# Two blocks' down projections joined into two levels of seven products, in a fused attention and SwiGLU kernel

## The chip, the cores and the metric

The kernel runs on one core of a Trainium2 chip. The metric is the device time of one execution in microseconds (us); a lower time is better. A profile shows one execution, and its span is the time from the first to the last instruction that the profiler saw.

## The reference

Attention without a softmax, normed by rows, feeds a SwiGLU feed-forward block. All is float32.

```python
kv = np.einsum('bhsd,bhse->bhde', k, v)          # 8 batches, 8 heads, 576 positions, 64 wide
out = np.einsum('bhsd,bhde->bhse', q, kv)
rms = np.sqrt(np.mean(out * out, axis=-1, keepdims=True) + 1e-06)
attn_out = out / rms * g_norm
x = attn_out.transpose(0, 2, 1, 3).reshape(4608, 512)
g = x @ w_gate                                   # 512 -> 1536
silu = g * (1.0 / (1.0 + np.exp(-g)))
result = (silu * (x @ w_val)) @ w_out            # 1536 -> 512
```

## The kernel before

The 4608 tokens are cut into nine blocks of 512. For each block, the attention makes x (transposed, features on the partitions), the *up phase* makes h = silu(x w_gate) * (x w_val), and the *down phase* makes h w_out. Matrix products are made by Strassen's scheme in Winograd's form: a product of 2 x 2 blocks takes seven block products, numbered 1 to 7, instead of eight, and sums and differences of blocks before and after. The names follow: `XO`, `XI`, `CHAIN` map a product's number to its operand and to its PSUM bank.

Blocks 0 to 2 go alone. Blocks 3 and 4, 5 and 6, 7 and 8 go in pairs (`Pair`). A pair's up phase (`Pair.up`, `Inner`) has two levels of seven products for both blocks at once. It runs in six steps j, one for each 256 columns of the gate and value weights (2 x 128 each). A step has the seven outer products in four groups: (1, 5), (6, 2), (7), (4, 3), called g0 to g3. Each group has seven inner products, and one of them is one matmul of 128x128 by 128x256 for each outer product in the group. A step has thus 49 matmuls. The 49 weights come from a DRAM tensor, `w`, through nine buffers `t` (`Stream.pump`), sent on SP's queue.

The inner products of a group share PSUM banks: 1, 6, 7 and 4 add up in a bank "b" (three buffers), 5 and 3 in a bank "c" (two), and 2 has a bank "a" (one). After each of them VectorE or ScalarE reads the bank, adds what is to be added, and writes a tile `r` in SBUF (L820 to L832); only then may the next product of the same bank begin. ScalarE does this for products 1, 5, 6 and 4 of g0, VectorE for all others. TensorE's order interleaves two groups: 1, 5, the last group's 3, 6, the last group's 4, 2, 7 (`Inner.sequence`, L798). GpSimd makes the outer sums (`made1` and `made2`: four sums of 128x256 and one of 128x1024 each step), and after g3's last product (`made3`, L852) two multiplies of 128x1024 that make h, and a sum and a difference of 128x256 for the first block of the pair (`h_sums`). In the sixth step VectorE makes the multiplies and these sums.

A block's down phase (`Ffn.down`, `Down`) has one level of seven products. Each has six steps of contraction and two row tiles: 12 matmuls of 128x128 by 128x256, h being the stationary operand, so that the output has tokens on the partitions and is stored in rows. The pair's two blocks go down one after the other, 14 products in all. The weights are quadrants of `wo` in SBUF and three differences, that GpSimd makes into `t` buffers (`turn_t`, L997). In the last two blocks (`lone`) product 3 comes ahead of 4 and has a bank "m"; in the last block (`final`) its halves are apart, one ahead of product 4 and one behind it, and each half is summed and stored by itself. The second block's sums of h are made by GpSimd during the first one's down phase (`second_sums`, L1252).

The order of the work is that of the program, which a scheduler lays out by priorities for each engine; `tc.issue_after(x)` puts what follows behind an instruction x in that order, and `in_order` (L135) fixes the program's order for the engines named. Each engine takes its own queue strictly in turn.

Of the kernel before, what the change touches and what calls it, by code (L numbers as in the profile page):

```python
# [14 lines left out]
P = 128  # L15
# [3 lines left out]
def kernel(  # L19
# [114 lines left out]
    @contextmanager  # L134
    def in_order(*engines):  # L135

        traced = nc.cur_bb.bb.instructions
        last = traced[-1]
        yield
        start = next(k for k in reversed(range(len(traced))) if traced[k] is last) + 1  # L140
        before = {}
        for i in traced[start:]:
            if engines and i.engine not in engines:
                continue
            if i.engine in before:
                tc.add_manual_dep(
                    i, before[i.engine].name,
                    mybir.DependencyInfo(mybir.DependencyClass.NoSync, mybir.DependencyReason.DATA), reason="order",
                )
            before[i.engine] = i  # L150

# [488 lines left out]
    class Quad:  # L640


        def __init__(self, steps):
            self.steps = steps
            self.ps, self.room = {}, None

            self.apart = {}

# [3 lines left out]
        def multiply(self, p):  # L652
            name, first = CHAIN[p]
            if first:
                tiles = [PSUMS[name].tile([P, 2, HB], F32, name=name) for _ in range(1 + (name in self.apart))]
                self.ps[name], self.apart[name] = tiles[0], tiles[-1]
            banks = self.ps[name], self.apart[name]
            for e, i in self.order(p):
                lhsT, rhs = self.operands(p, e, i)

                self.ffn.multiplied = nc.tensor.matmul(  # L661
                    banks[e][:, e], lhsT=lhsT, rhs=rhs, start=first and i == 0 and (e == 0 or banks[0] is not banks[1]),
                    stop=i == self.steps - 1, skip_group_check=True,
                )
            getattr(self, f"after{p}", lambda: None)()
# [91 lines left out]
    class Inner:  # L757
# [94 lines left out]
        def made3(self, p, e, q):  # L852
            if p != 4:
                return
            h = h_both[:, :, 2 * self.j : 2 * self.j + 2]
            halves = lambda t: t.rearrange("p (b e) t -> p b e t", b=2)
            c11, c12, c21, c22 = (self.whole(*i) for i in ((1, 1), (3, 1), (3, 0), (1, 0)))

            engine = nc.gpsimd if self.j + 1 < NP else nc.vector
            mul(engine, h[:, :, :, 0:HB], halves(c11), halves(c12))  # L860
            with tc.issue_after(self.ffn.fifth.ins):
                nc.scalar.activation(out=c21, in_=c21, func=ACT.Silu)
            mul(engine, h[:, :, :, HB:BLK], halves(c21), halves(c22))
            self.ffn.ended = self.ffn.a.h_sums(self.j, 1, engine)

# [13 lines left out]
    class Stream:  # L879
# [15 lines left out]
        def pump(self):  # L895

            while self.next and not self.held[-9]:
                n, j, c = key = self.next.pop(0)
                tile_ = t_tile(key)
                os, ps = JOINT[c]  # L900
                count = len(os) * len(ps)
                self.tiles[key] = tile_.rearrange("p a (b c) -> p (a b) c", c=P)
                self.uses[key] = count
                to = self.tiles[key][:, 0:count].rearrange("p (o i) c -> p o (i c)", o=len(os))
                src = self.dram[:, j, steps_of(OUTERS, os), steps_of(INNERS, ps)].rearrange("p o i c -> p o (i c)")
                nc.sync.dma_start(out=to, in_=src)

        def use(self, n, j, o, p):
            c, i = self.joint[o, p]
            key = n, j, c  # L910
            self.uses[key] -= 1
            if not self.uses[key]:
                self.free(key)
            return self.tiles[key][:, i]
# [4 lines left out]
    stream = Stream()  # L919
# [65 lines left out]
    class Down(Quad):  # L985
        def __init__(self, ffn):
            super().__init__(NP)
            self.ffn = ffn
            self.t = {}
            self.final = ffn.n == NB - 1  # L990
            self.lone = False
            self.opens = None
            self.keeps = False
            if self.final:
                self.apart["c"] = None
# [16 lines left out]
        def multiply(self, p, es=(0, 1)):  # L1012
            if p == 3 and self.lone:
                self.third(es)
                return
# [7 lines left out]
        def third(self, es):  # L1023


            if es[0] == 0:
                tiles = [m_psum.tile([P, 2, HB], F32, name="m") for _ in range(1 + self.final)]
                self.thirds = tiles[0], tiles[-1]
            for e in es:
                for i in range(self.steps):  # L1030
                    lhsT, rhs = self.operands(3, e, i)
                    self.ffn.multiplied = nc.tensor.matmul(  # L1032
                        self.thirds[e][:, e], lhsT=lhsT, rhs=rhs, start=i == 0 and (e == 0 or self.final),
                        stop=i == self.steps - 1, skip_group_check=True,
                    )
            if not self.final:
                add(nc.vector, self.o1[:, :, HD:DM], self.thirds[0], self.u2)
                self.ffn.store(self.o1, 0)
                return
            for e in es:  # L1040
                add(nc.vector, self.o1[:, e, HD:DM], self.thirds[e][:, e], self.u2[:, e])
                self.ffn.store(self.o1[:, e : e + 1, HD:DM], e, slice(HD, DM))

        def after6(self):
            super().after6()
            if self.lone:
                self.add_c(self.u2, self.u2)

        def order(self, p):
            order = [(e, i) for e in range(2) for i in range(self.steps)]  # L1050
            return order if p == 3 and self.final else sorted(order, key=lambda ei: ei[1])
# [17 lines left out]
        def rows(self):  # L1069
            o = ring()  # L1070
            self.o1, self.o2 = o[:, 0:2], o[:, 2:4]

        def after2(self):
            if self.lone:
                self.rows()
            add(nc.vector, self.o1[:, :, 0:HD], self.ps["a"], self.s)
            if self.final:
                self.ffn.store(self.o1[:, :, 0:HD], 0, slice(0, HD))
# [4 lines left out]
        def after7(self):  # L1083
            if not self.lone:
                self.rows()
            u3 = self.piece(2)
            nc.scalar.copy(out=u3, in_=self.ps["b"])
            self.add_c(self.o2[:, :, HD:DM], u3)
# [5 lines left out]
        def after3(self):  # L1094
            self.add_c(self.o1[:, :, HD:DM], self.u2)
            if not self.final:
                self.ffn.store(self.o1, 0)
                return
            for e in range(2):
                self.ffn.store(self.o1[:, e : e + 1, HD:DM], e, slice(HD, DM))  # L1100

        def add_c(self, o, u):

            if not self.final:
                add(nc.vector, o, self.ps["c"], u)
                return
            for e, c in enumerate((self.ps["c"], self.apart["c"])):
                add(nc.vector, o[:, e], c[:, e], u[:, e])

    class Ffn:  # L1110
# [9 lines left out]
        def store(self, o, t, columns=slice(None)):  # L1120
            rows = out[BLK * self.n : BLK * (self.n + 1), columns].rearrange("(t p) d -> p t d", t=T)
# [40 lines left out]
        def down(self, nxt, then={}):  # L1162
# [3 lines left out]
            down.lone = nxt is None  # L1166
            order = (1, 6, 5, 7, 2, 4, 3) if 5 in fill else (1, 5, 6, 7, 2, 4, 3)
            if down.lone:
                order = (1, 5, 6, 2, 7, 3, 4)
            for p in order:  # L1170
# [5 lines left out]
                with tc.issue_after(nxt.multiplied.ins) if self.n == 0 and p in (5, 6) else ExitStack():  # L1176
                    down.multiply(p, *[(0,)] * (p == 3 and down.lone and down.final))
# [14 lines left out]
            if down.lone and down.final:  # L1192
                down.multiply(3, (1,))
# [25 lines left out]
    class Pair:  # L1219


        def __init__(self, n):
            self.n = n
            self.a, self.b = (Ffn(i, blocks[i]) for i in (n, n + 1))
            self.visited = None

        def up(self, fill):

            a = self.a
            a.s1 = s_pool.tile([P, NP, HB], F32, name="s1")  # L1230
# [5 lines left out]
            for i, this in enumerate(units):  # L1236
                for unit, p in this.sequence(last):
                    if unit:
                        visited, self.visited = self.visited, None
                        with tc.issue_after(visited.ins) if visited else ExitStack():  # L1240
                            unit.multiply(p)
                last = this
                fill.get(i + 1, lambda: None)()
            a.down_ = Down(a)
            a.down_.keeps = True
            a.down_.turn_t(5)
# [3 lines left out]
            a.ended = self.ended  # L1250
# [165 lines left out]
    for n in range(PAIRED, NB, 2):  # L1416
# [3 lines left out]
        if after:  # L1420
# [10 lines left out]
            for i in range(8):  # L1431
                fill[12 + i] = lambda i=i, after=after: after[i // 4].load_quarters(i % 4 // 2, (i % 2,))
        pair.up(fill)
        if after:
            after[0].turn()
        if len(after) > 2:
            after[2].load_kv(0)
        with in_order(nc.tensor.engine):
            pair.a.down(after[0] if after else None, {5: pair.second_sums})
            if after:  # L1440
                after[1].turn()
            if len(after) > 2:
                after[2].load_kv(1)
            pair.b.down(after[1] if after else None)
# [31 lines left out]
```

## Time and profile before

| | us |
|---|---|
| median of three runs | 1012.57 (1011.34 to 1013.79) |
| the profiled execution, its own time | 1012.7 |
| its span | 1010.9 |
| TensorE busy | 993.7 (98%) |
| VectorE busy | 673.7 (67%) |
| GpSimd busy | 369.6 (37%) |
| ScalarE busy | 232.2 (23%) |
| last up phase (blocks 7 and 8), from about 808 to | 934.85 |
| the two down phases behind it, to TensorE's last matmul | 1007.55 |

In the profile PE is TensorE, PEld its weight loads, DVE is VectorE, ACT is ScalarE, POOL is GpSimd and SP is the engine whose queue sends most of the DMAs. A row of a group of instructions gives the line of the code, the engine, the operation, the tile written and the tiles read, the shape and the count; most sums have the lines of three helpers, L130 (add), L131 (subtract) and L132 (multiply). A matmul of float32 shows as two records. A transfer's "us to landing" is the time from its issue to the arrival of its data.

### The profile page before, as it was taken

Reading aid. Unit: us, or ns where it says so; the run is one execution under the profiler, and the core shown is the slowest. Engines: PE = TensorE matmul, PEld = TensorE weight load, DVE = VectorE, ACT = ScalarE, POOL = GpSimd, SP = SyncE. Lnnn points to the kernel's source line nnn. Section 1 sums busy time; section 2 is a strip of 40 time slices with the busy share of each in tenths; the row PEclk is TensorE's granted clock in tenths of the full one; section 3 lists DMA queues with packets and bytes.
Section 4 is the critical chain, followed back from the end, with each engine's and each line's share of the span. In section 5 each row is a group of like instructions: output and inputs, shape, how many; then the busy total and the mean of one; then the engine's idle time right before and its main releaser. Section 6 shows DMA issues by size and latency. Waiting matters only on the chain.

```text
span 1010.9 us, 17078 instructions
## 1 busy us (share of the span) xinstructions
PE 993.7 (98%) x6506; PEld 831.6 (82%) x6506; DVE 673.7 (67%) x1121; ACT 232.2 (23%) x367; POOL 369.6 (37%) x290
## 2 busy tenths in 40 slices
PE   5999999999999999999999999999999999999998
PEld 4544688888888888888888888888888888888887
DVE  2999797589868477656676746666668566666311
ACT  2665111221122311212211121121112121121000
POOL 0000263255544240445456004455660026546600
PEclk9999999999999999999999999999999999999999
DMA  8688653483866855767742464667221654553011
GB/s 220 198 266 260 120 93 136 97 288 97 210 136 122 214 114 158 189 179 182 170 130 42 111 164 135 182 164 191 77 42 43 146 164 144 150 145 101 1 42 42
DMA packets 254290, 143.23 MB, mean 142 GB/s; under 512 B 149504, under 2 KB 236544, under 8 KB 254208
## 3 DMA queue, kind: packets, MB, share of 16 engines
q1 hardware_dynamic: 223488, 138.20, 50.8%
q10 hardware_dynamic: 30656, 3.94, 2.5%
q8 instruction: 52, 0.85, 0.4%
q14 instruction: 30, 0.25, 0.1%
q0 software_dynamic: 64, 0.00, 0.0%
HBM read 104.99 MB, written 28.70 MB: 132 GB/s over the span
## 4 chain that ended last, share of the span: by engine, by line
PE 75%; DMA 1%; POOL 0%; SPq 0%; issue 0%; DVE 0%; POOLq 0%
PE b L816 22%; PE b L661 20%; PE c L816 11%; PE c L661 9%; PE a L816 5%; PE a L661 5%; PE m L431 1%; PE m L1032 1%; PE m L370 1%; DMA ld<-in_v_dram 1%; POOL t L131 0%; SPq L312 0%; PE b L370 0%; PE b L431 0%; PE a L431 0%
## 5 line engine op out<-in xcount | busy, mean ns | idle before, releaser
L816 PE MATMUL b<-arena,t 128*128 128x256 f32 x1008 | 244.5, 381 | 0.0
L816 PEld LDWEIGHTS b<-arena,t 128*128 128x128 f32 x1008 | 190.1, 190 | 29.6 <-DVE r L130 2.4
L130 POOL TENSOR_TENSOR r<-r 128x256 f32<-128x256 f32 (+1 forms) x90 | 94.7, 1054 | 246.1 <-DVE r L130 154.9
L130 DVE TENSOR_TENSOR r<-b,r 128x512 f32<-128x512 f32 (+1 forms) x234 | 138.9, 606 | 60.1 <-PE b L816 54.8
L130 DVE TENSOR_TENSOR r<-c,r 128x512 f32<-128x512 f32 (+1 forms) x170 | 104.5, 623 | 81.9 <-PE c L816 40.1
L132 POOL TENSOR_TENSOR arena<-r 128x1024 f32<-128x1024 f32 (+1 forms) x54 | 102.1, 1904 | 112.3 <-DVE r L130 67.9
L131 POOL TENSOR_TENSOR t<-wo 128x512 f32<-128x512 f32 x54 | 76.9, 1445 | 167.8 <-DVE wo L130 105.9
L130 DVE TENSOR_TENSOR r<-a,r 128x512 f32<-128x512 f32 x93 | 59.2, 636 | 108.3 <-PE a L661 70.7
L816 PE MATMUL c<-arena,t 128*128 128x256 f32 x504 | 122.5, 379 | 0.0
L131 DVE TENSOR_TENSOR arena<-arena 128x512 f32<-128x512 f32 (+3 forms) x96 | 104.3, 1101 | 20.0 <-PE b L661 17.7
L816 PEld LDWEIGHTS c<-arena,t 128*128 128x128 f32 x504 | 95.6, 190 | 13.5 <-issue 0.3
L661 PE MATMUL b<-wo,arena 128*128 128x256 f32 x432 | 98.1, 382 | 0.2
L661 PE MATMUL b<-t,arena 128*128 128x256 f32 x432 | 96.2, 379 | 0.0
L661 PEld LDWEIGHTS b<-wo,arena 128*128 128x128 f32 x432 | 81.2, 190 | 12.5 <-DVE arena L132 0.9
L661 PEld LDWEIGHTS b<-t,arena 128*128 128x128 f32 x432 | 82.1, 190 | 11.2
L830 ACT COPY r<-b 128x512 f32<-128x512 f32 x54 | 31.7, 586 | 189.9 <-PE b L816 189.9
L131 POOL TENSOR_TENSOR t<-arena 128x512 f32<-128x512 f32 x36 | 51.1, 1432 | 56.2 <-PE c L661 21.9
L816 PE MATMUL a<-arena,t 128*128 128x256 f32 x252 | 66.1, 379 | 0.0
L816 PEld LDWEIGHTS a<-arena,t 128*128 128x128 f32 x252 | 47.9, 190 | 6.5
L661 PE MATMUL c<-t,s 128*128 128x256 f32 x216 | 48.1, 379 | 0.0
L661 PE MATMUL a<-wo,arena 128*128 128x256 f32 x216 | 48.1, 379 | 0.0
L661 PEld LDWEIGHTS a<-wo,arena 128*128 128x128 f32 x216 | 41.0, 190 | 5.6
(115 smaller groups left out, 1242.9 us busy)
## 6 DMA issues: line engine op xcount, KB each, us to landing
t<-w SPq DMA_DIRECT2D x180, 256.0 KB, 3.1
out_dram<-r SPq DMA_DIRECT2D x17, 512.0 KB, 2.9
ld<-in_k_dram SPq DMA_DIRECT2D x26, 288.0 KB, 4.6
ld<-in_v_dram SPq DMA_DIRECT2D x26, 288.0 KB, 6.1
t<-w SPq DMA_DIRECT2D x54, 128.0 KB, 2.3
ld<-in_moe_w_gate_dram SPq DMA_DIRECT2D x12, 512.0 KB, 4.6
ld<-in_moe_w_val_dram SPq DMA_DIRECT2D x12, 512.0 KB, 4.7
ld<-in_moe_w_out_dram SPq DMA_DIRECT2D x12, 512.0 KB, 4.8
```

The lines of the kernel that those rows point to most:

```text
L130: add = lambda e, o, a, b: e.tensor_tensor(out=o, in0=a, in1=b, op=OP.add)
L131: sub = lambda e, o, a, b: e.tensor_tensor(out=o, in0=a, in1=b, op=OP.subtract)
L132: mul = lambda e, o, a, b: e.tensor_tensor(out=o, in0=a, in1=b, op=OP.mult)
L370: self.positions = nc.tensor.matmul(self.kv_ps[r][u * D : (u + 1) * D, g, :], lhsT=k[:, u, c, :], rhs=v[:, u, c, :], start=(c == 0), stop= ...
L431: self.multiplied = nc.tensor.matmul(self.ps[i][u][p : p + D, t, j, :], lhsT=self.qt[rows, tile_t, head, p : p + D], rhs=kvs[b % 3][rows, ...
L661: self.ffn.multiplied = nc.tensor.matmul(banks[e][:, e], lhsT=lhsT, rhs=rhs, start=first and i == 0 and (e == 0 or banks[0] is not banks[1 ...
L816: self.ffn.multiplied = nc.tensor.matmul(ps[:, i], lhsT=stream.use(self.ffn.n, self.j, o, p), rhs=self.operand(o, p), start=first and i == ...
L830: copied = nc.scalar.copy(out=dst, in_=ps)
L1032: self.ffn.multiplied = nc.tensor.matmul(self.thirds[e][:, e], lhsT=lhsT, rhs=rhs, start=i == 0 and (e == 0 or self.final), stop=i == self ...
```

## The change

The last pair has an object `deep`. Its two blocks go down together, by two levels of seven products (49), each with three matmuls (the contraction in three steps c) of 128x128 by 128x256; the weights are the stationary operand now, and the 256 columns are 128 tokens of each block. The output has features on the partitions and has to be turned before it is stored.

In the pair's up phase the weights' sums are made ready. After every second inner product, `tick` takes one step of a list and puts it on VectorE directly behind the last VectorE instruction of the program so far (`behind`): six sums on `wo`; for each of nine leaf blocks a difference of 128x512, two differences of 128x128 and 128x256 and, at the next tick, a send of 128x896 to a DRAM tensor `leaf`, with three empty ticks behind it, as there is a single buffer for them; twelve differences of 128x384 kept in SBUF. `turn` adds eight sums of 128x512 on h, each due 26 ticks' counts after its multiplies. All of these read two tiles in SBUF. In steps 0 to 4, GpSimd makes its sum and difference of h for both blocks, 128x512 each; the ones of `turn_t`, `second_sums` and the tile s1 of the last pair fall away.

In the joint down phase (`Deep.down`) the order of TensorE and of VectorE is the program's. VectorE makes the outer sums of h (`outer`), the extras of the inner level (`sum_x`, 128x768 each) and the sums behind the products. Two of the four quarters of the output are turned in blocks of 32x32 by VectorE, and 32 stores in runs of 128 bytes set the blocks in place, 16 on ScalarE's queue and 16 on SP's. The other two are turned by TensorE, 16 transposes of 128x128, copied by ScalarE and, for the last, VectorE, and stored by SP.

```diff
+    def behind(engine):
+        return tc.issue_after(next(i for i in reversed(nc.cur_bb.bb.instructions) if i.engine == engine))
...
             mul(engine, h[:, :, :, 0:HB], halves(c11), halves(c12))
+            if self.ffn.deep:
+                self.ffn.deep.made(self.j, engine, c21, halves(c21), halves(c22), h)
+                return
...
+    class Last(Inner):
+        GROUPS = ((1, 2), (6, 5), (7,), (4, 3))
...
+            for c in cs:
+                for i, o in enumerate(self.outers):
+                    self.ffn.multiplied = nc.tensor.matmul(
+                        ps[:, i], lhsT=self.deep.weight(o, p, c), rhs=self.deep.operand(o, p, c),
+                        start=first and c == 0 and i == 0, stop=c == 2, skip_group_check=True,
+                    )
+            stream.pump()
...
+    class Deep:
...
+        def turned_block(self, i, c):
...
+            def differences():
+                sub(nc.vector, temp[:, 4], temp[:, 0], temp[:, 1])
+                sub(nc.vector, temp[:, 5:7], temp[:, 2:4], temp[:, 1:2].to_broadcast([P, 2, P]))
+            def send():
+                nc.sync.dma_start(out=self.dram[:, i, c], in_=temp[:, 0:7])
+            return [lambda: sub(nc.vector, raw, b, t2o), differences, send, None, None, None]
...
+        def tick(self):
+            self.count += 1
+            if self.count % 2:
+                return
+            steps = self.later
+            if self.due and self.due[0][0] <= self.count:
+                steps = [self.due.pop(0)[1]]
+            step = steps.pop(0) if steps else None
+            if step:
+                with behind(nc.vector.engine):
+                    step()
+        def made(self, j, engine, c21, g, v, h):
+            def second():
+                mul(engine, h[:, :, :, HB:BLK], g, v)
+                a11, a21, a22 = h[:, :, 0, 0:HB], h[:, :, 0, HB:BLK], h[:, :, 1, HB:BLK]
+                add(engine, a21, a21, a22)
+                sub(engine, a21, a21, a11)
...
+            second()
+            if j % 2:
+                self.due += [(self.count + 26, step) for i in range(2) for step in self.turn(j // 2, i)]
...
+        def sum_x(self, x, *os):
...
+        def outer(self, o, parts=((0, 0), (0, 1), (1, 0), (1, 1))):
...
+        def send(self, room, half, cols, queue):
...
+                    for r in range(4):
+                        dst = out[row : row + HB, col + 32 * r : col + 32 * (r + 1)]
+                        queue.dma_start(
+                            out=dst.rearrange("(c i) j -> i c j", i=32), in_=t[32 * r : 32 * (r + 1), f, e]
+                        )
+        def turn_back(self, e, q, final=False):
+            ps = m_psum.tile([P, 2, 2, P], F32, name="m")
...
+                    nc.tensor.transpose(ps[:, o, f], self.shared[3][:, o, f, e, q], ident)
...
+            if final:
+                for o in range(2):
+                    nc.vector.tensor_copy(out=to[:, o], in_=ps[:, o])
+            else:
+                nc.scalar.copy(out=to, in_=ps)
...
+        def down(self):
...
+            m(3, 6)
+            add(nc.vector, c22, u3, c22)
+            m(3, 5)
+            nc.vector.transpose(out=room[:, 1], in_=c22)
+            self.send(room[:, 1], 1, 1, nc.sync)
+            m(3, 2)
+            m(3, 7)
+            self.rows = ring().rearrange("p (e q) (o f d) -> p e q o f d", e=2, o=2, f=2)
+            m(3, 3)
+            self.turn_back(0, 0)
+            self.turn_back(1, 1)
+            m(3, 4)
+            self.turn_back(1, 0)
+            self.turn_back(0, 1, True)
...
+                    if self.deep:
+                        deep.tick()
...
+        if pair.deep:
+            stream.leaves(pair.deep)
+            pair.up(fill)
+            with in_order(nc.tensor.engine, nc.vector.engine):
+                pair.deep.down()
+            continue
```

What served only the last two blocks in `Down` and `Quad` (`lone`, `final`, `third`, `apart`, the stores by columns) is taken out; for the other blocks it makes no difference to the instructions.

## The prediction

> **What bounds the kernel now.** I read the busy shares first, then the 40 slices, then the chain that ended last, and last the windows and the timeline of the last 200 us, the only stretch whose program differs.
>
> ```profile
> PE 993.7 (98%) x6506; PEld 831.6 (82%) x6506; DVE 673.7 (67%) x1121; ACT 232.2 (23%) x367; POOL 369.6 (37%) x290
> PE   5999999999999999999999999999999999999998
> DVE  2999797589868477656676746666668566666311
> POOL 0000263255544240445456004455660026546600
> PEclk9999999999999999999999999999999999999999
> ```
>
> TensorE is never short of work between the first and the last slice, at the full granted clock. So only two things shorten the run: fewer TensorE passes, or a shorter tail; and any wait put on TensorE lengthens it by its whole length.
>
> ```profile
> 871.91:893.06 21.15, 21.15 (x100) 18.62 (x99) 14.16 (x24) 4.46 (x7) 11.40 (x9) 1.00 0.51 152
> 934.85:1007.55 72.70, 72.69 (x337) 63.66 (x335) 16.34 (x19) 5.75 (x9) 16.29 (x12) 1.00 0.07 26
> ```
>
> These are two stretches (columns: length, then busy time of PE, PEld, DVE, ACT, POOL). The first is one of the six steps j of the last up phase: 49 matmuls in 21.15 us, 0.432 us each. VectorE is busy 14.2 us of it and GpSimd 11.4, so VectorE has 7.0 us free, but GpSimd runs beside it more than half of the time. The second is the two down phases of blocks 7 and 8: 14 products of 12 matmuls, 168 x 0.432 = 72.6 us, with VectorE and GpSimd nearly idle.
>
> ```profile
> 992.00 5.18 PE b L661 x24
> 997.18 2.59 PE m L1032 x12
> 999.77 5.18 PE b L661 x24
> 1004.95 2.60 PE m L1032 x12
> ```
>
> The end of the chain in order of time (start, length): the end is TensorE's. A matmul of float32 leaves two records, so "x24" is 12 matmuls, 5.18 us. After 1007.55 come one VectorE sum (0.42 us) and a store; the span ends at 1010.9, so the tail is 3.3 us.
>
> [...] In the weight stage (VectorE first, then GpSimd):
>
> ```profile
> 223.83 1.35 DVE L131 TENSOR_TENSOR t<-t 128x128 f32<-128x128 f32 x1
> 225.22 0.29 DVE L130 TENSOR_TENSOR t<-t 128x128 f32<-128x128 f32 x1
> ```
>
> ```profile
> 222.21 1.54 POOL L132 TENSOR_TENSOR arena<-r 128x512 f32<-128x512 f32 x1 [2.18 <-DVE t L130]
> 223.72 1.31 POOL L131 TENSOR_TENSOR t<-wo 128x512 f32<-128x512 f32 x1
> ```
>
> The same 128x128 sum takes 0.29 us alone and 1.35 us when it comes just after a GpSimd instruction began: it waits until about 0.13 us before that one's end. Some fifty VectorE sums of that stage show it, up to 1.07 us more each, and of two VectorE sums in a row each waits for a new GpSimd instruction. The sums that read PSUM stay at 0.69 us whatever GpSimd does. [...] Sums in a row follow each other 0.08 us faster (0.61 us at 512).
>
> **The change, part by part.**
>
> *Products of the down phase.* 7 x 7 leaf products of 3 matmuls of 128x256 replace 168 matmuls: 147 x 0.432 = 63.5 us, so -9.1 us. Against it 16 transposes of 128x128; the first stage shows them 0.109 us apart. 8 stand between the last two products (+0.9 us), 8 in the tail.
>
> *Tail.* After the last product: sum 0.69, four transposes 0.63, two copies 0.75 (0.42 + 0.33), about 0.15 of handing over, then the store and the end as now, 2.9: 5.1 us against 3.3, so +1.8. Together -9.1 + 0.9 + 1.8 = -6.4 us if TensorE never waits.
>
> *VectorE in the joint down phase.* It gets 21 sums of extras and 12 outer sums at 0.87 us (29 us), the sums of the products (6 of 512 and 4 of 256 in the first two groups, 3 more of 512, 7 of 256, 7 of 512: some 13 us), and some 10 us of multiplies, leaf sums, wide sums and two block transposes (1.22 us each): 53 us in 64. GpSimd is done by then, so nothing is locked. I put the two queues next to each other in the built order, product by product: the extras of group (1, 2) are ready at 940.0, product 5 needs them at 942.6; those of (6, 5) at 955, needed at 958; the last group (4, 3) gets its sums one product ahead. No wait comes out; the least room is some 0.4 us. I take 0, bound 3.
>
> *Stores.* 32 transfers of 32 KB in runs of 128 bytes, on ACT's and SP's queues, and 8 of 128 KB. [...] loads of q of 32 KB in the same runs take 2.3 us here against 2.3 for 128 KB of t<-w. [...] ACT's begin near 986 and are out near 996, before its first copy of transposes (997); SP's begin near 990 and are out near 1000, before the last stores. They are hidden with little to spare: 0, bound 3.
>
> *Side sums of the last up phase.* These decide. VectorE gets 53 sums of two SBUF inputs: 6 on wo (512 columns), for each of nine leaf blocks 512, 128 and 256, 12 kept differences of 384, 8 turns of h of 512. Alone they cost 23 x 0.61 + 9 x 0.34 + 9 x 0.20 + 12 x 0.48 = 24.7 us, 4.1 per step: they would fit into the 7.0 us free. But each stands in VectorE's queue in front of the sum that empties the next PSUM bank, and GpSimd's sums of h double (s and arena of 128x256, 0.73 us each, become 128x512, 1.27 us by the rows of the down phase), 12.5 us busy per step. In the built order I took the step of 871.91, whose timeline reads (GpSimd, then VectorE)
>
> ```profile
> 874.89 4.69 POOL L132 TENSOR_TENSOR arena<-r 128x1024 f32<-128x1024 f32 x2 [3.80 <-DVE r L130]
> ```
>
> ```profile
> 874.93 0.69 DVE L130 TENSOR_TENSOR r<-a,r 128x512 f32<-128x512 f32 x1 [0.18 <-PE a L816]
> 876.65 0.69 DVE L130 TENSOR_TENSOR r<-b,r 128x512 f32<-128x512 f32 x1 [0.16 <-PE b L816]
> 879.18 0.69 DVE L130 TENSOR_TENSOR r<-b,r 128x512 f32<-128x512 f32 x1 [0.17 <-PE b L816]
> ```
>
> and put in the sums of the third step (j = 2). The first stands behind the sum of 874.93 and is reached at 875.54; GpSimd's first multiply (2.36 us) ends at 877.25, so it ends at 877.80. The sum that was at 876.65 then ends at 879.02. Product 6 of that group adds onto the same bank and would start at 878.12: TensorE waits 0.95 us. The two differences behind it wait for the second multiply (to 880.03) and for the sum of h after it (to 881.3) and end at 881.6; three bank sums later, at 883.3, the one of 879.18 is done, for which product 7 waits: from 881.66 on, 1.75 us. The later ones of the step meet GpSimd's short sums: 0.85 us. In all 3.6 us. In the same way: j = 0, GpSimd idle at first, 1.2; j = 1, whose first sum comes three products later, 1.5; j = 3, two turns and a raw sum, 2.4; j = 4, with kept differences, 3.7; j = 5, the same with more of them, 3.8. Sum 16 us. The trace shows waits for GpSimd instructions of 1.3 us, none for one of 2.36; if a wait ends at 1.07 us, and GpSimd doesn't come in between two differences, it is 10 us. Above, leaf writes of 448 KB (3.5 us to land by the row of 384 KB) that hold up the next raw sum: 4 us more. From below nothing: a VectorE sum can't make TensorE faster here. I take 16.
>
> *The new waits' followers.* Behind a held VectorE sum stand all bank sums, and behind these TensorE's products 6 and 7 of each group (products 5 and 3 of other groups, 1.7 us of work, lie between); GpSimd's adds come later too, but have room. On SP nine leaf writes stand among the weight loads and 21 leaf loads of 192 KB replace none; DMA is half busy. 0.
>
> Sum: -6.4 + 16 = +9.6 us on the profiled execution (span 1010.9, its time 1012.7, 0.1 above the median 1012.57): 1012.6 + 9.6 = about 1022.
>
> **Rivals.** (1) The lock costs TensorE nothing: faster. The mechanism: the banks' slack (a bank sum of 0.69 us in 1.7 us of other products) and the free 7 us absorb the waits. For it: in the weight stage fifty such waits left TensorE without gaps; against it: there the products between are twice as long (1.73 us each), and here waits come in pairs. It wins below 6.4 us of waits, measurably below 4.4; with none it gives 1012.6 - 6.4 = 1006.2. (2) The milder lock, 10 us or less: 1016, and about level with 6. (3) The down phase becomes VectorE's: with 0.1 us more on each of its 65 instructions it has 60 us in 64, and the room of 0.4 us is gone in places; +3 to any case. (4) The small stores hold up the last ones: +3. That the change doesn't do what it says I exclude: the built order has the 147 matmuls, and each side sum behind the named sum.
>
> **Chances.** Waits of 10 to 20 us, 1016 to 1026: 0.58, likeliest 1022. Milder, 1011 to 1016: 0.19. Rival 1, below 1011: 0.16, nearly all of it a gain beyond 0.2%. Above 1028 or so, with rivals 3 and 4 on top: 0.05. Range 1011 to 1028. About 0.2% (2 us) is what a measurement of this kernel can tell from no change: faster 0.16, same 0.11, slower 0.73.
>
> **What would show it.** Windows of the last up phase: steps of 21.15 us grow to 22.5 to 25, the third, fifth and sixth most, with TensorE idle in front of products 6 and 7, released by VectorE. Side sums of 128 columns take 1.0 us and more in GpSimd's stretch. The joint down takes about 64.5 us to the last product with no idle TensorE, and the tail 5.1 us. I am wrong if the steps stay at 21.2 us, or if the time is lost in the down phase or behind stores.

## The result, and the profile after

The changed kernel takes 1018.36 us (median of seven runs, 1015.85 to 1020.51) against 1012.05 us for the kernel before, measured beside it. The ratio is 1.0063, with a 95% interval of 1.0047 to 1.0078. The forecast was 1022 us and slower, with a range of 1011 to 1028.

The profiled execution has a span of 1016.1 us, 5.2 us above that of before. The busy shares and slices of its page, the rows shown for the kernel before:

```profile
PE 990.6 (97%) x6480; PEld 824.1 (81%) x6480; DVE 746.7 (73%) x1227; ACT 233.2 (23%) x370; POOL 360.5 (35%) x275
PE   5999999999999999999999999999999999999997
DVE  2999797589778577656686656666767588889894
POOL 0000273345444231544654005554660046555000
```

TensorE is busy 3.1 us less, VectorE 73.0 us more. The slices are too coarse for the loss: one of 25 us still reads 9 with 2.4 us of idle time in it. So I cut the windows at TensorE's own landmarks: the six steps of the last up phase, each from the start of g0's product 2 to the next one (the sixth ends with the same kind of product in the joint down phase), then the joint down phase to its last product, and the tail. The columns are those of the prediction's windows.

```profile
809.08:830.31 21.23, 21.23 (x99) 18.54 (x98) 18.26 (x33) 3.98 (x6) 5.93 (x5) 1.00 0.57 178
830.31:851.66 21.35, 21.35 (x100) 18.50 (x99) 16.90 (x30) 4.46 (x6) 13.01 (x9) 1.00 0.68 212
851.66:875.23 23.57, 22.11 (x99) 18.29 (x98) 20.09 (x32) 4.46 (x6) 13.19 (x9) 1.00 0.56 176
875.23:898.81 23.58, 21.69 (x100) 18.43 (x98) 19.74 (x32) 4.46 (x6) 13.65 (x9) 1.00 0.57 176
898.81:922.62 23.81, 21.95 (x100) 18.37 (x98) 22.17 (x35) 4.46 (x6) 13.37 (x9) 1.00 0.51 156
922.62:946.35 23.73, 21.70 (x95) 17.36 (x94) 21.41 (x34) 2.70 (x3) 13.84 (x9) 1.00 0.42 122
946.35:1009.36 63.01, 63.01 (x297) 55.12 (x296) 53.06 (x70) 5.97 (x11) 0.00 (x0) 1.00 0.25 60
1009.36:1016.10 6.74, 1.06 (x8) 0.61 (x6) 1.45 (x3) 0.59 (x1) 0.00 (x0) 0.94 0.50 141
```

The time is lost in the third to sixth steps. The first two take about the 21.15 us of before. In the joint down phase TensorE never idles; VectorE is busy 53.06 us of it. The tail is 6.7 us instead of 3.3. The sixth window is a little short of a full step, since the next landmark lies early in the down phase; without idle time it is 20.48 us long (run e1_psum below), so the stalls of the six steps are 0.1 + 0.2 + 2.4 + 2.4 + 2.7 + 3.2 = 11.0 us.

The waits of TensorE in this stretch (what waited, for whom, total, times, longest) name one releaser:

```profile
PE b L817 <- DVE r L130: 7.2, 10, 1.1
```

All are products on bank b that wait for the sum on VectorE that reads this bank. (The 7.2 us count from modelled ends of matmuls and leave out the slower record after each stall, 0.32 us in place of 0.216; the lengths of the windows are the safer measure.) The third step shows what kept that sum. VectorE, then GpSimd, then TensorE:

```profile
853.40 2.26 DVE L131 TENSOR_TENSOR s<-wo 128x512 f32<-128x512 f32 x1
855.58 1.27 DVE L130 TENSOR_TENSOR r<-b,r 128x512 f32<-128x512 f32 x2
856.78 1.57 DVE L131 TENSOR_TENSOR s<-s 128x128 f32<-128x128 f32 x2
```

```profile
852.75 5.12 POOL L132 TENSOR_TENSOR arena<-r 128x1024 f32<-128x1024 f32 x2 [3.28 <-DVE r L130]
857.95 1.54 POOL L130 TENSOR_TENSOR arena<-arena 128x512 f32<-128x512 f32 x1
```

```profile
852.52 1.89 PE L817 MATMUL b<-arena,t 128*128 128x256 f32 x8
...
856.91 1.99 PE L817 MATMUL b<-arena,t 128*128 128x256 f32 x8 [0.78 <-DVE r L130]
...
860.40 0.91 PE L817 MATMUL b<-arena,t 128*128 128x256 f32 x3 [0.64 <-DVE r L130]
```

The side sum s<-wo needs 0.68 us alone and takes 2.26 us, because GpSimd's multiply began 0.65 us before it and lasts 2.36 us. The bank sums behind it in VectorE's queue read PSUM; the matmuls that fill their bank (852.52) had ended at 854.41, but they start only at 855.58, when the side sum is done, and product 6 comes 0.93 us late. The two differences (1.57 us in place of 0.62) do the same to product 7. GpSimd pays too: its second multiply, which found VectorE's side sum in progress, took 2.80 us, so that the two show 5.12 us instead of 4.69.

### The profile page after: what moved, and what is told of

It reads as the page before. It is cut to its first block, busy times and chain, and to the rows that moved or that the text cites. A ratio compares the mean times of both kernels' runs of the same rounds, so it can differ in the third digit from the quotient of the medians.

```text
span 1016.1 us, 17218 instructions
## 1 busy us (share of the span) xinstructions
PE 990.6 (97%) x6480; PEld 824.1 (81%) x6480; DVE 746.7 (73%) x1227; ACT 233.2 (23%) x370; POOL 360.5 (35%) x275
## 4 chain that ended last, share of the span: by engine, by line
PE 73%; DVE 3%; issue 1%; DVEq 0%
PE b L817 21%; PE b L662 16%; PE c L817 10%; PE c L662 8%; PE a L817 5%; PE a L662 4%; PE b L893 4%; PE c L893 2%; DVE r L130 2%; PE m L435 1%; PE a L893 1%; PE m L374 1%; DVE s L131 0%; DVE arena L131 0%; PE b L374 0%
## 5 line engine op out<-in xcount | busy, mean ns | idle before, releaser
L817 PE MATMUL b<-arena,t 128*128 128x256 f32 x1008 | 246.5, 382 | 7.2 <-DVE r L130 7.2
L130 DVE TENSOR_TENSOR r<-b,r 128x512 f32<-128x512 f32 (+1 forms) x247 | 145.2, 602 | 61.1 <-PE b L817 50.4
L131 DVE TENSOR_TENSOR arena<-arena 128x512 f32<-128x512 f32 (+4 forms) x121 | 124.1, 1043 | 9.2 <-PE b L662 6.9
L131 POOL TENSOR_TENSOR t<-wo 128x512 f32<-128x512 f32 x45 | 64.2, 1447 | 162.9 <-DVE wo L130 105.4
L662 PE MATMUL b<-wo,arena 128*128 128x256 f32 x336 | 76.8, 382 | 0.2
L662 PE MATMUL b<-t,arena 128*128 128x256 f32 x336 | 74.8, 379 | 0.0
L662 PEld LDWEIGHTS b<-wo,arena 128*128 128x128 f32 x336 | 62.9, 190 | 10.1 <-DVE arena L132 0.9
L662 PEld LDWEIGHTS b<-t,arena 128*128 128x128 f32 x336 | 63.8, 190 | 8.7
L662 PE MATMUL b<-arena 128*128 128x256 f32 x192 | 45.5, 380 | 0.0
L662 PE MATMUL b<-arena,t 128*128 128x256 f32 x192 | 45.4, 379 | 0.0
L1464 PE MATMUL b<-arena 128*128 128x512 f32 (+1 forms) x104 | 43.5, 561 | 0.5 <-ACT arena L499 0.5
```

What stands on the lines that cost most here:

```text
L130: add = lambda e, o, a, b: e.tensor_tensor(out=o, in0=a, in1=b, op=OP.add)
L131: sub = lambda e, o, a, b: e.tensor_tensor(out=o, in0=a, in1=b, op=OP.subtract)
L662: self.ffn.multiplied = nc.tensor.matmul(ps[:, e], lhsT=lhsT, rhs=rhs, start=first and i == 0 and e == 0, stop=i == self.steps - 1, skip_g ...
L817: self.ffn.multiplied = nc.tensor.matmul(ps[:, i], lhsT=stream.use(self.ffn.n, self.j, o, p), rhs=self.operand(o, p), start=first and i == ...
L1464: nc.tensor.matmul(t, lhsT=w[f // 2][:, i, P * (f % 2) : P * (f % 2 + 1)], rhs=x[:, i, of], start=(i == 0), stop=(i == NS - 1),)
```

## Experiments

The theory: the stalls come from side sums with two SBUF inputs that wait for a whole GpSimd instruction, with ready bank sums queued behind them. The wait for GpSimd's instruction in progress is called the lock here, as in the prediction. The rivals: VectorE's queue is simply too long; or the binding of each side sum to its place costs the time. For each run I give the stalls of the six steps, worked out as above. Each ratio is to the kernel before, measured beside that run; runs that were not measured together are compared by these ratios and by their traces.

**e1_psum: the same side sums, second operand in PSUM.**

```diff
-            return [lambda: sub(nc.vector, raw, b, t2o), differences, send, None, None, None]
+            return [lambda: sub(nc.vector, raw, b, self.flat(2)), differences, send, None, None, None]
...
+            self.still = m_psum.tile([P, BLK], F32, name="m")
+            nc.tensor.matmul(self.still, lhsT=ident, rhs=wo[:, 0], start=True, stop=True)
```

The other side sums (differences, kept differences, sums on wo, turns) have the same edit.

> Changed computation: the side sums of the last up phase that are made of two SBUF tiles read, in place of the second one, a PSUM tile that is filled once (0.9 us of TensorE), so the last two blocks' output is not the reference's; shapes, count and places of the instructions stay. Lock theory (the stalls of the last up phase come from VectorE instructions with two SBUF inputs that wait for GpSimd): the side sums go at their own 0.3 to 0.7 us whatever GpSimd does, the steps of 23.6 us fall back to 21.3 or so, the time falls by some 9 us to about 1009. Queue rival (the stalls come from the mere length of VectorE's queue, 4 us more in every step in front of the bank sums): steps stay at 23.6 us, time about 1018. In both the tail stays at 6.7 us.

Measured: 1008.92 us, ratio 0.995 (0.9934 to 0.9965). From VectorE and then GpSimd in the same place:

```profile
856.39 0.68 DVE L131 TENSOR_TENSOR s<-wo,m 128x512 f32<-128x512 f32 x1
...
858.18 0.60 DVE L131 TENSOR_TENSOR s<-s,m 128x128 f32<-128x128 f32 x2
```

```profile
855.74 4.69 POOL L132 TENSOR_TENSOR arena<-r 128x1024 f32<-128x1024 f32 x2 [3.29 <-DVE r L130]
```

The side sum stands at the same point of the multiply and takes 0.68 us; the multiplies take their 4.69 us again. The middle four steps are 21.15 or 21.16 us, and no stall is left. VectorE has as many instructions as in the changed kernel (1227), in the same order but for two bank sums next to each other that changed places. The queue rival is out.

**e2_window: the same sums, placed where GpSimd is idle.** The tick now looks at the product it follows, and not at a count:

```diff
+        SLOT = {(3, 1): "b", (2, 3): "b", (2, 4): "o", (0, 5): "oo", (3, 3): "b", (3, 4): "b"}
+        def tick(self, g, p):
...
+            for kind in self.SLOT.get((g, p), ""):
+                if kind == "b" and self.blocks:
+                    self.block()
+                elif self.due and self.due[0][0] <= self.count:
+                    self.run(self.due.pop(0)[1])
+                elif self.free:
+                    self.run(self.free.pop(0))
...
```

The keys are a group and a product; "b" is a step of a leaf block, "o" a turn or a kept difference. A leaf block's differences follow one tick after its raw difference.

> The same side sums, but placed by the product they follow: behind products of g3, g2 and g0's 5, where GpSimd is idle between its multiplies and its outer sums; the first step as it was. Lock theory: the side sums don't meet GpSimd, steps of 21.2 to 21.8 us in the second to sixth, time about 1008 to 1010, below both kernels. Queue rival (their sum counts, not their place): about 1018, or later if they bunch.

Measured: 1007.28 us, a little below what I expected, ratio 0.994 (0.9928 to 0.9953): faster than both kernels. Windows of the third and fourth step:

```profile
854.49:875.65 21.16, 21.16 (x100) 18.62 (x99) 18.14 (x34) 4.46 (x6) 12.84 (x9) 1.00 0.62 194
875.65:896.80 21.15, 21.15 (x100) 18.62 (x99) 18.45 (x34) 4.46 (x6) 12.95 (x9) 1.00 0.64 199
```

The stalls sum to 0.5 us. Durations of the leaf blocks' raw differences (minimum/median/maximum in ns), first of the changed kernel, then of this one:

```profile
L131 DVE TENSOR_TENSOR s<-wo x9: 676/683/2261, 817.7 to 900.5; 128x512 f32<-128x512 f32 x9
```

```profile
L131 DVE TENSOR_TENSOR s<-wo x9: 676/681/694, 820.3 to 896.5; 128x512 f32<-128x512 f32 x9
```

The medians are alike and the maxima tell; of the smaller differences none takes more than 0.42 us here, where the longest took 1.26. A few long waits make the loss, so a median would have hidden it.

**e5_nobehind: the binding undone.**

```diff
             if step:
-                with behind(nc.vector.engine):
-                    step()
+                step()
```

> The side sums are not bound to the place behind the last VectorE instruction of the program; the scheduler is free to put them. Lock theory: what counts is where they fall against GpSimd's multiplies; they now bunch in the early part of the last up phase, so stalls move to other steps; some 6 to 14 us of stalls in all, time 1014 to 1022. If the binding itself costs the time (a side sum held in front of ready bank sums): stalls go, about 1009.

Measured: 1027.65 us, ratio 1.0136 (1.0118 to 1.0154); the stalls are 22.8 us, more than I expected. Some 5 us of them are matmuls at a granted clock of 0.50 behind three long stalls (last section). The worst place, VectorE and then TensorE:

```profile
858.93 0.69 DVE L131 TENSOR_TENSOR s<-wo 128x512 f32<-128x512 f32 x1 [5.08 <-DMA leaf<-s]
...
863.88 2.81 DVE L130 TENSOR_TENSOR arena<-arena 128x512 f32<-128x512 f32 x1 [1.93 <-POOL arena L132]
```

```profile
867.95 3.78 PE L817 MATMUL b<-arena,t 128*128 128x256 f32 x8 [5.68 <-DVE r L130]
```

Unbound, a raw difference stands at the head of VectorE's queue before its buffer is free and waits 5.08 us for the leaf's write; a turn waits 1.93 us for a multiply's result and then 2.1 us for the second multiply. Bank sums that are ready wait behind both. So the binding doesn't cost the time, it saves some: it puts each side sum where its data is there. What it doesn't see is GpSimd.

**e7_halves: GpSimd's multiplies in two halves each.**

```diff
-                mul(engine, h[:, :, :, HB:BLK], g, v)
+                if j + 1 < NP:
+                    for b in range(2):
+                        mul(engine, h[:, b, :, HB:BLK], g[:, b], v[:, b])
...
```

The first multiply has the same edit.

> GpSimd's multiplies of 128x1024 in the last up phase are each split in two of 128x512, so that one lock lasts 1.3 us instead of 2.36. Lock theory, with the wait ending 0.1 us before the end of the GpSimd instruction in progress: the first stall of each step from the third on (0.95 us, product 6 of the group behind the multiplies) mostly goes, later stalls shrink a little or stay; steps of 22.3 to 23 us, time about 1013 to 1016. If the wait is for GpSimd's work as a whole (it goes on as long as GpSimd has instructions in a row): no change, 1018 or more, since GpSimd's two more instructions cost it about 0.2 us each.

Measured: 1018.97 us, ratio 1.005 (1.0034 to 1.0065): no gain that can be told from the changed kernel, where I expected 1013 to 1016. The first stall of the third step did go, as the lock theory has it, but the stalls still sum to 10.0 us. VectorE and GpSimd:

```profile
856.38 1.17 DVE L131 TENSOR_TENSOR s<-wo 128x512 f32<-128x512 f32 x1
...
858.67 2.80 DVE L131 TENSOR_TENSOR s<-s 128x128 f32<-128x128 f32 x2
```

```profile
855.73 5.46 POOL L132 TENSOR_TENSOR arena<-r 128x512 f32<-128x512 f32 x4 [3.29 <-DVE r L130]
```

The raw difference now takes 1.17 us, but the two differences take 2.80 (1.39 + 1.48) in place of 1.57: each waits for a half multiply of its own. Product 7 comes 2.0 us late, where it was 0.8. The time alone would fit the other theory, a wait for GpSimd's work as a whole; the trace rules it out: the raw difference ends at 857.55, 0.55 us after the first half multiply (857.00), while GpSimd goes on with the other halves until 861.19.

**e9_halves_one: halves, and the two differences in one instruction.**

```diff
-                sub(nc.vector, temp[:, 4], temp[:, 0], temp[:, 1])
-                sub(nc.vector, temp[:, 5:7], temp[:, 2:4], temp[:, 1:2].to_broadcast([P, 2, P]))
+                sub(nc.vector, temp[:, 4:7], temp[:, 1:4], temp[:, 0:1].to_broadcast([P, 3, P]))
```

> The multiplies split in two as in the earlier run with halves, and the two differences of a leaf block (128x128 and 128x256) made as one instruction of 128x384 with other operands, so the last two blocks' output is not the reference's. Theory: with halves, GpSimd starts its next instruction between the two differences, so each waits a whole instruction, and that ate the gain; with one instruction only one wait is left: steps of 22 to 22.5 us, time about 1011 to 1014. If the second stall has another cause (the number of sums in front of product 7): as with halves, 1018 or so.

Measured: 1016.3 us, ratio 1.0037 (1.0023 to 1.005). The steps are 22.5 to 23.2 us and the stalls 7.7 us, 2.3 less than with two differences. The sign is right, the size half of what I expected or less: the third step gains 1.2 us and the fifth 1.1, the others nothing, and product 7 still waits 0.85 us in the third. In the time the intervals of the two runs overlap; only the trace tells them apart.

**e8_hhalf: GpSimd's sums of h at their old size.**

```diff
-                add(engine, a21, a21, a22)
-                sub(engine, a21, a21, a11)
+                those = slice(0, 2 if j == NP - 1 else 1)
+                add(engine, a21[:, those], a21[:, those], a22[:, those])
+                sub(engine, a21[:, those], a21[:, those], a11[:, those])
```

> GpSimd's sum and difference of h are made for the first block of the pair alone (128x256, 0.7 us, instead of 128x512, 1.3 us), as they were before the change; the second block's are left out, so its output is not the reference's. If the doubled sums of h are part of the stalls (step of the prediction: the differences wait for a sum of h as well): the second stall of a step, 0.8 to 1.3 us, falls by 0.4 us or more, time about 1014 to 1016. If the stalls come from the two multiplies alone: steps stay at 23.6 us, 1018.

Measured: 1019.27 us, ratio 1.0071 (1.0055 to 1.0086); steps of 23.5 to 23.8 us, stalls 10.9 us as against 11.0. The doubled sums of h cost nothing here: the prediction's step that the differences wait for one of them fails.

**e3_nosmall: no small stores.**

```diff
             nc.vector.transpose(out=room[:, 0], in_=c11)
-            self.send(room[:, 0], 0, 0, nc.scalar)
...
-            self.send(room[:, 1], 1, 1, nc.sync)
```

> Leaves out the 32 small stores, so two of the four quarters of the last two blocks' output are not written; all else as in the changed kernel. If the small stores hold up the last ones (rival 4): the first large store goes out when its copy is ready, 1 us earlier, and the last issues and landings shorten too; the tail falls from 6.7 or 5.6 us to some 4.5. If they are hidden: the first large store earlier, the last ones as before, tail 5.6, time 1017 to 1018.

Measured: 1019.41 us, ratio 1.0067 (1.0053 to 1.0081). The first large store goes out 0.03 us after its copy, and not 1 us after it as in the changed kernel; but the tail, 7.2 us, is not shorter. Its length alone says little, since SP's last issue took 1.99 us here. The start of that issue is the better measure: 2.60 us after the last product without the small stores, 2.61 with them. So the small stores do delay the first large one, and this is hidden.

**e6_both: e2_window, and the last product in two parts.**

```diff
-            m(3, 4)
+            m(3, 4, (0,))
             self.turn_back(1, 0)
+            m(3, 4, (1, 2))
```

> The side sums placed where GpSimd is idle, as in the run with windows, and the last product made in two parts: its first third of the contraction, then the transposes and the store of the quarter that is ready, then the other two thirds. Lock theory with a tail set by the last stores: steps stay at 21.3 us, the stores of the third quarter are issued 0.9 us earlier and only two 128 KB stores remain behind the last product; tail 4.5 to 5 us instead of 5.6, time about 1006. If the last store's own issue and landing set the tail: unchanged, 1007.

Measured: 1007.51 us, ratio 0.9949 (0.9937 to 0.9961), no better than e2_window by ratio; the 1006 that I expected did not come. The tail is 5.8 us, as against 5.6. But in the profiled execution the stores of the third quarter did not go out earlier: an issue of 1.38 us stood ahead of them in SP's queue, and they were issued 1.15 and 1.63 us after the last product, where e2_window has 1.08 and 1.50. So this trace does not test what earlier stores would bring.

## Why the prediction was right in sign and too high

**Products of the down phase, -9.1 + 0.9 us.** Right. From g0's product 2 in the first step to the last product, the kernel before takes 1007.55 - 810.26 = 197.3 us and e1_psum 1001.58 - 812.26 = 189.3 us: -8.0, where the sum had -8.2. The whole effect with next to no stalls is e2_window's: 0.6% of 1012.57, or 6 us, gained.

**VectorE in the joint down phase, 0.** Right: TensorE's busy time fills the 63.01 us window, with VectorE at 53.06, where I had 53 in 64. Rival 3 didn't come. The 0.87 us for a sum of 768 columns, and the 0.48 us for a side sum of 384, were estimates: the trace of before has no VectorE sum of these widths, only 0.69 us at 512 columns and 1.22 at 1024. The changed kernel's 33 sums of 768 columns take 0.95 us each and start 0.87 us apart in a row; a kept difference of 384 that GpSimd doesn't hold up takes 0.54 us, and the next instruction starts 0.47 us after it.

**Small stores, 0; rival 4, +3.** Hidden (e3_nosmall). On the way there the prediction gave each queue some 10 us for its 16. In the changed kernel each queue issues them in a row, 0.5 us apart, in 8 us, with no idle time between them; a store lands 1.7 us after its issue.

**Tail, +1.8.** A little low. It is +2.3 in e2_window (5.6 us) and +3.4 in the profiled execution of the changed kernel. The chain after the last product is as I had it; its last pieces in the changed kernel (a sum, four transposes, the first of two copies):

```profile
1009.39 0.70 DVE r L130
...
1010.23 0.64 PE m L1080 x4
...
1010.90 0.42 DVE r L1084
```

But the last of four stores in a row stands behind the one before it in SP's queue and starts 0.3 us after its copy, a term the sum had left out. The other 1.1 us are one long issue: the last store's took 1.13 us where the others take 0.4 to 0.5, and the span ends 4.1 us after it began, against 3.0 in e2_window. Such an issue came up in some executions and not in others; why is open.

**Side sums, 16 us, lower value 10.** The mechanism is right and is shown: lock, held bank sums, late products 6 and 7. Beside a multiply of 2.36 us the raw difference of two SBUF tiles took 2.26 us; with one SBUF input and one in PSUM it took 0.68 us at the same point (e1_psum). The size is wrong: the stalls are 11.0 us. Step by step, predicted and measured:

| j | 0 | 1 | 2 | 3 | 4 | 5 |
|---|---|---|---|---|---|---|
| predicted, us | 1.2 | 1.5 | 3.6 | 2.4 | 3.7 | 3.8 |
| measured, us | 0.1 | 0.2 | 2.4 | 2.4 | 2.7 | 3.2 |

In the worked step the first stall was 0.95 predicted, 0.93 measured: the wait for a multiply of 2.36 us goes on to its end (2.26 us in place of 0.68, 1.58 more), not to 1.07. The second was 1.75 predicted and 0.80 measured. The term that failed is the sum of h behind the second multiply, for which the differences were to wait (to 881.3). In the changed kernel none of the nine second differences waits: each takes 0.41 us. The first difference ends its wait when the multiply ends, the second comes right behind it at 857.94, and GpSimd's next sum begins at 857.95, finds VectorE ahead, and takes 1.54 us in place of 1.27. The margin of 0.01 us is thin, but the same at all three places of this kernel where GpSimd's next sum or difference of h follows so closely (837.86, 857.95 and 905.10). e7_halves shows the other outcome, where the next half multiply had begun at 859.86, before the second difference at 859.98. Why the one comes in and the other not is argued from these starts (GpSimd's sum of h needs the multiply just done, the next half multiply doesn't), not shown.

For j = 0 and 1 the waits exist (in the first a difference of 1.26 us, in the second a raw difference and a difference held by half a microsecond each), but the bank sums behind them are done in time, all but 0.1 and 0.2 us: waits of up to 1 us were absorbed here by the work of the products between. I had counted those two steps "in the same way" as the third without finding the product that would be late. That makes 2.4 of the 5 us too many.

**Sum.** From the first step's landmark: -8.0 + 11.0 + 3.4 = +6.4 us; the part ahead of it happened to be 1.2 us shorter in this execution than in that of before (809.08 against 810.26), which leaves the 5.2 us between the spans. In the medians it is +6.3. That the total came out 3.6 us from the forecast owes something to luck: the waits were 5 us too high, and the tail 1.6 too low, 1.1 of it the one long issue. The waits of 11.0 us lie at the low end of the main case and near the 10 us of rival 2. Of the two conditions of rival 2 one held (GpSimd does not come in between two differences) and one did not (a wait ends at 1.07 us). Rival 1, in which the waits cost TensorE nothing, held for the first two steps only.

## What to carry to other kernels

Before free time on VectorE is filled with sums of two SBUF tiles, look at where GpSimd is busy, and not at how much time is free: the same 53 sums cost 11 us in one place and 0.5 in another. What counts is the ready work queued behind the instruction that waits, and each such wait has to be followed to the product that it makes late. Where the place can't be chosen, an operand in PSUM avoided the lock (e1_psum, 0.68 us where the sum of two SBUF tiles took 2.26); splitting GpSimd's instruction gained little (e7_halves, 10.0 us of stalls), since several sums then waited in turn.

## What had not been expected of the hardware

After the stall of 5.7 us in e5_nobehind eight matmul records took 3.78 us (the TensorE row shown there), 0.43 us from one to the next, where 0.216 is usual. The same came in the second and the fifth step, where TensorE was idle for 3.1 us in each (lengths 26.20 and 26.19 us, busy 23.07 and 23.11). The windows over these records give the granted clock (the figure after the engines) as 0.50:

```profile
838.19:841.60 3.41, 2.91 (x7) 2.38 (x8) 3.41 (x5) 0.00 (x0) 3.25 (x3) 0.50 0.00 0
865.49:872.32 6.83, 4.37 (x10) 3.53 (x11) 6.63 (x9) 0.55 (x1) 3.52 (x3) 0.50 0.12 39
920.11:923.52 3.41, 3.41 (x10) 2.66 (x9) 3.31 (x5) 0.58 (x1) 0.36 (x1) 0.50 0.30 84
```

TensorE worked for 2.91 + 4.37 + 3.41 = 10.7 us at a granted clock of 0.50, so by my estimate some 5.3 us of the run's 22.8 us of stalls are not waiting, but slow work behind it. The low stretches lasted 3.41, 6.83 and 3.41 us. The first two began in a stall, 0.50 and 2.46 us before work went on; in the third TensorE was busy from the first moment, so there the low clock came when the waiting was over. What sets it off was not shown. After stalls of about 1 us in the changed kernel the granted clock stayed 1.00 (the six steps' windows), and only the first record was stretched, to 0.32 us.

SP's issue of a store of 128 KB, 0.4 to 0.5 us otherwise, took 1.13, 1.38, 1.94 and 1.99 us, once each in four of the profiled executions (the changed kernel, e6_both, e9_halves_one, e3_nosmall).
